# An mLSTM cell with a SwiGLU block behind it: the steps of the beginning in another order, and the last group's results stored in token order

## The chip, the cores and the metric

One core of one Trainium2 chip. Times are device microseconds. The kernel before took 580.2 us (median of three runs, 579.98 to 581.21). A profile of one execution has a span of 577.6 us from the first to the last instruction; all positions below are microseconds from the start of that span. The profile's names: PE is TensorE (matmul), PEld its weight loads, DVE VectorE, ACT ScalarE, POOL GpSimd, SP the engine that issues most DMAs.

## The reference

The attention part is a recurrence over 768 tokens for 4 x 8 heads of 40 elements; the second part is a SwiGLU block on 3072 tokens of 320 features, with 1536 hidden units.

```python
for t in range(S):                                   # B=4, H=8, S=768, D=40
    m_new  = maximum(f_gate[t] + m, i_gate[t])
    f_stab = exp(f_gate[t] + m - m_new); i_stab = exp(i_gate[t] - m_new); m = m_new
    C = f_stab * C + i_stab * outer(v[t], k[t])      # D x D per head
    n = f_stab * n + i_stab * k[t]
    y[t] = sigmoid(o_gate[t]) * (C @ q[t]) / maximum(abs(n @ q[t]), 1.0)
x = y.transpose(0, 2, 1, 3).reshape(B * S, H * D)    # 3072 x 320
g = x @ w_gate                                       # 320 x 1536
out = (g * sigmoid(g) * (x @ w_val)) @ w_out         # 3072 x 320, float32
```

The three weight matrices come as 64-bit floats, and the kernel turns them into 32-bit ones itself.

## The kernel before

The recurrence is done in chunks of 128 tokens. A *unit* is one chunk of one batch (24 units, 6 per batch), a *group* is three units, 384 tokens; there are eight groups. Every group goes through the SwiGLU block in twelve hidden blocks of 128 columns (`H`), then three output tiles of 128 tokens (`J`).

Every step is a Python generator that records a few instructions each time it is advanced, and a string says in which order the generators are advanced. The instructions then stand in that order on every engine, and each engine works in order. `START` is the string of the beginning: the gates, the attention of the first six units, the loads and conversion of all weights, and the whole SwiGLU block of group 0. Later groups have their own strings, which the change leaves alone.

```python
START = """
bar0 pad2 pad3 R1 R0*4 kq0 kq2 pad4 pad2 pad1 pad0 bar0 C1 kq0 runA decA*2 pad1 runB tgA tgB tgA R1*3 kq0 mp which kq0 M0 T0 kq1 M0 ...
"""                                                  # (cut)

def play(names, streams):
    for name in names.split():
        name, _, n = name.partition("*")
        for _ in range(int(n or 1)):
            next(streams.get(name, iter(())), None)
    for s in streams.values():
        do(s)
```

The steps by name (a number is a unit, or a piece of the weights):

- `runA`, `runB`: the two scans over the gates for the first and the second three chunks (`A` on 128 rows, `B` on 32). `mp`, `ep`: split of the running maxima and of the decays into three bf16 parts. `tgA`, `tgB`: transpose of the gates on TensorE and copy to `g_T`. `decA`, `decB`: the decays between chunks. `which`: small constants. `pad`: memsets of the rings. `store`: maxima and decays to DRAM (`M_dram`, `e_dram`).
- `kq`, `v`, `o`: loads. `bar`, `M`: the maxima of a unit spread over TensorE's accumulators (tile `mb`); `W`: exponentials of them (tile `w_sb`). `w`: the same maxima read from DRAM instead, one broadcast of 512 KB. `T`: transpose of k and q. `E`/`e`: the decays, on TensorE or from DRAM (`e_bc`). `S`: scores (`sp`), times `w_sb`, and q times the decay.
- `P`, `I`: the two parts of y (`yT`). `N`: the new state C (`add`). `F`: division, output gate, and the transpose into `xT`.
- `R`: loads of a piece of the weights into one of five raw buffers; `B`: loads of the "behind" slice, the weight rows of features 32 to 39 of every head, into the end of `h_ring`. `C`: conversion of a piece (two ACT, two DVE, one POOL instruction).

The parts that the change touches, or that the working below needs:

```python
def convert(n):                                       # C
    ...
    nc.scalar.activation(bits, hi.bitcast(F32), AF.Abs, scale=2.0 ** -112)
    nc.scalar.activation(low, lo, AF.Identity, scale=2.0 ** -29, bias=step_c)
    yield
    nc.vector.tensor_scalar(bits, bits, scalar1=3, scalar2=None, op0=ALU.logical_shift_left)
    nc.vector.scalar_tensor_tensor(size, in0=hi, scalar=0x80000000, in1=bits, op0=ALU.bitwise_and, op1=ALU.bitwise_xor)
    yield
    nc.gpsimd.tensor_tensor(place(*key).bitcast(U32), low, size, op=ALU.add)
    yield

def hidden(g, m, i0=0, i1=GC):                        # H
    cols = slice(i0 * L, i1 * L)
    ps = [psum.tile([128, TW], F32, name="gv_ps", tag="gen") for _ in range(2)]
    for kc in range(NKC):                             # 5 slices, the fifth is the "behind" slice
        for i in range(2):
            r = slice(i * HP, (i + 1) * HP)
            nc.tensor.matmul(ps[i][:, cols], lhsT=wgv_sb[r, kc, ts(m, 128)], rhs=xts[g][r, kc, cols], ...)
    yield
    sg = gsp.tile([128, TW], F32, name="sg")
    nc.scalar.activation(sg[:, cols], ps[0][:, cols], AF.Sigmoid if g else AF.Silu)
    yield
    if g:
        nc.vector.tensor_tensor(sg[:, cols], sg[:, cols], ps[0][:, cols], op=ALU.mult)
    nc.vector.tensor_tensor(h_ring[:, (g * NFC + m) % NH, cols], sg[:, cols], ps[1][:, cols], op=ALU.mult)
    yield

def project_last(g, i):                               # last output tile of the last group
    n = DM // 2
    for c, mul in enumerate((nc.scalar.mul, nc.vector.tensor_scalar_mul)):
        p = psum.tile([128, n], F32, name="o_ps", tag="gen")
        for m in range(NFC):
            nc.tensor.matmul(p, lhsT=h_ring[:, (g * NFC + m) % NH, ts(i, 128)], rhs=wo["sb"][:, m, ts(c, n)], ...)
        yield
        z = gsp.tile([128, n], F32, name="z_sb")
        mul(z, p, 1 / TWICE)
        yield
        dst = out[ds(g * TW + i * 128, 128), ts(c, n)].rearrange("(t four) d -> four t d", four=NSQ)
        for r in range(NSQ):
            (nc.sync if r % 2 else nc.scalar).dma_start(out=dst[r], in_=z[r * 32:(r + 1) * 32])
        yield
```

Within a tile of 128 tokens, `xT`, `h_ring` and the results stand in the order "four t": token 0, 4, 8, ..., then 1, 5, ... A store puts the rows back in their places. For group 0, blocks 0 to 2 are done in two parts, of 128 columns (first unit) and of 256 (the other two), so that there are fifteen `H` steps there.

Of the kernel before, what the change touches and what calls it, by code (L numbers as in the profile page):

```python
# [13 lines left out]
ALU = mybir.AluOpType  # L14
# [18 lines left out]
"""  # L33

START = """
bar0 pad2 pad3 R1 R0*4 kq0 kq2 pad4 pad2 pad1 pad0 bar0 C1 kq0 runA decA*2 pad1 runB tgA tgB tgA R1*3 kq0 mp which kq0 M0 T0 kq1 M0 bar1 decB pad0 M1 W0 ep tgB M1 o0 o2 C2 pad5*2 W0 T0*3 store C1 v0 kq1 bar2 pad3 M2 B M2 kq2 o0 v1 W0 R5*3 decB C2 R5 kq1*2 o2 o1 S0 decA o1 C2 store S0 pad4 T1 kq2 v2 B S0 kq2 W1 B*2 decB C1 W1 T2 w3 R2*2 W1 kq3 I0 W2 T1 R2 T2 kq3 kq4 decA R2 G0 F0 C7 G2 N0 decA kq4 R3 kq5*2 decB G0 N0 R4 T1 kq5*2 kq4 decB T1 N1*2 G1 kq4 F0 N1 S1 kq3*2 R3*3 R4*3 C7 W2 F0 G2 S1*2 W2 T2 B F0 E1 T2 C7 F0 W3 C0 S1 S2 C0 W3 B*3 S2 G1 P1 W3 R7 I1 E2 C0 C3 S2 F1 H0 S2 R7 H0 T4 F1 P2 T3 R7 store v3 R7 F1 I2 T4 T3 T5*2 R10 T5 C3 F2 R10 F2 R10 R6 F1 R6 T4 F2 H0 R6 F1 C3 T5 T4 R6 F2 N2 C4 T3 H1 F2 o5 H4 H1 C4 C6 C4 N2 R10 H4 H1 R11 C6 o3 T3 R8 H4 C6 R11*2 H5*2 R11 H2 N2 H2 H5 C5*2 R8 C8 R8 C5 H2 S3 C8*2 C10*2 H7 R8 R9 C10 C13*2 W3 H7 C13 H8 H7 C9 H8 C9 R9 C14 R9 H8 C9 o3 R9 C14 C15 C14 S3 H6*2 H3 H6 N3 C11 R16 C15 H3*2 C11 N3 R18 w4 G3 C15 H10 N3 R17 C11 e3 C12*2 v4 C12 e3 H14 C20 H10 S3 R12 C22 e4*2 S4 R15 C20 H10 R13 W4 H14 C20 C22 W4 H14 W4 H13 G3 H9 W4 o5 R14 H13 H9 S4 C22 o4 C21 H13 H11 C19 S4*2 C21 H9 H11 C21 C16 R19 H12 C19 C16 H11 w5 S3 C19 C17 P3 C16 C17 N4*3 H12 C18*2 C17 C18 C23 I3 G5 W5 v7 C23 w8 e5 S5 W5 C23 e5 v5 W5 G5 X o4 J0 H12 F3 S5 w6 S5*2 J1 W8 X J2 F3 J2 W8 G4 P5 x0 P4 w7 x0*2 F3 I5 X I4 x0*3 F5 v8 J6 v6 x2 x0 J3 F3 J2 F3 W7 G4 W8 X W7 x2 F4 F5 F4*2 x2 F5 W6 W8 W7 x0 F5 J7 x2 J4 x2 x3 F4 W7 k6*2 x1 x2 x1 F4 J8*3 F5 x3 x1 x2 k7 W6 J5 W6 x3 J5*2 x1*2 k7 W6 x1*2 x3 x1 x3 k8*2 x3*3 x2
"""


# [16 lines left out]
def kernel(  # L56
# [25 lines left out]
    nc = tc.nc  # L82
    B, H, S, D = q.shape
# [7 lines left out]
    NFC = DF // 128  # L91
    GC = NB // 2
    TW = GC * L
    HP = 64
    NKC = DM // HP
    NG = 2 * B
# [20 lines left out]
    for c0, c1, quarters in ((0, GC, (0, 2, 3)), (GC, NB, (0,))):  # L117
        for r in quarters:
            for t, a in ((f_sb, f_gate), (i_sb, i_gate)):
                (nc.scalar if r else nc.sync).dma_start(  # L120
                    out=t[r * BH:(r + 1) * BH, c0:c1], in_=a.rearrange("b h (c t) -> (b h) c t", t=L)[:, c0:c1])
# [3 lines left out]
    NSQ = L // 32  # L125
# [6 lines left out]
    NH = NFC + 1  # L132
    h_ring = const.tile([128, NH, TW], F32)
# [86 lines left out]
    X = 2 * D  # L220
    wgv_sb = wpool.tile([128, NKC, DF], F32)
    wo = {}
    N4 = 4
    P4 = DF // N4
# [441 lines left out]
    def hidden(g, m, i0=0, i1=GC):  # L666

        cols = slice(i0 * L, i1 * L)
        ps = [psum.tile([128, TW], F32, name="gv_ps", tag="gen") for _ in range(2)]
        for kc in range(NKC):  # L670
            for i in range(2):
                r = slice(i * HP, (i + 1) * HP)
                nc.tensor.matmul(ps[i][:, cols], lhsT=wgv_sb[r, kc, ts(m, 128)], rhs=xts[g][r, kc, cols],  # L673
                                 start=(kc == 0), stop=(kc == NKC - 1))
# [3 lines that stand above are left out]
        yield  # L678
        if g:
            nc.vector.tensor_tensor(sg[:, cols], sg[:, cols], ps[0][:, cols], op=ALU.mult)  # L680
        nc.vector.tensor_tensor(h_ring[:, (g * NFC + m) % NH, cols], sg[:, cols], ps[1][:, cols], op=ALU.mult)  # L681
        yield

    def project(g, i, part):

        if part == 0:
            tag = "conv" if g and i < 2 else "gen"
            hs[g, i] = psum.tile([128, DM], F32, name="o_ps", tag=tag, bufs=PB[tag])
        p = hs[g, i]
        n = NFC // 3  # L690
        for m in range(part * n, (part + 1) * n):
            nc.tensor.matmul(p, lhsT=h_ring[:, (g * NFC + m) % NH, ts(i, 128)], rhs=wo["sb"][:, m, :],  # L692
                             start=(m == 0), stop=(m == NFC - 1))
        yield
        if part == 2:
            z = gsp.tile([128, DM], F32, name="z_sb")
            nc.scalar.mul(z, p, 1 / TWICE)  # L697
            yield
            nc.sync.dma_start(out=out[ds(g * TW + i * 128, 128), :].rearrange("(t four) d -> four t d", four=NSQ), in_=z)
            yield  # L700

    def project_last(g, i):
# [5 lines that stand above are left out]
                nc.tensor.matmul(p, lhsT=h_ring[:, (g * NFC + m) % NH, ts(i, 128)], rhs=wo["sb"][:, m, ts(c, n)],  # L708
                                 start=(m == 0), stop=(m == NFC - 1))
            yield  # L710
            z = gsp.tile([128, n], F32, name="z_sb")
            mul(z, p, 1 / TWICE)
            yield
            dst = out[ds(g * TW + i * 128, 128), ts(c, n)].rearrange("(t four) d -> four t d", four=NSQ)
            for r in range(NSQ):
                (nc.sync if r % 2 else nc.scalar).dma_start(out=dst[r], in_=z[r * 32:(r + 1) * 32])
            yield


# [45 lines left out]
    for n, b in enumerate(blocks):  # L765
        stream(f"H{n}", hidden, 0, *b)
    for i in range(GC):
        for part in range(3):
            stream(f"J{3 * i + part}", project, 0, i, part)
# [3 lines left out]
    for g in range(1, NG):  # L773
        streams.clear()
        for m in range(NFC):
            stream(f"H{m}", hidden, g, m)
        for n in range(3 * GC):
            if g == NG - 1 and n >= 3 * (GC - 1):
                stream(f"J{n}", project_last, g, GC - 1)
                break  # L780
            stream(f"J{n}", project, g, *divmod(n, 3))
        for n, u in enumerate(group(g + 1)):
            for name, f in (("o", load_o), ("G", gate_o), ("e", load_e), ("S", scores), ("F", finish)):
                stream(f"{name}{n}", f, u)
            tag = "gen" if n < 2 else "cell"
            stream(f"N{n}", newer, u, "conv")
            stream(f"I{n}", within, u, tag, u % NB == 0)
            stream(f"P{n}", before, u, tag, True)
        for n, u in enumerate(group(g + 2)):
            for name, f in (("k", load_k), ("v", load_v), ("w", load_w), ("T", turn_x), ("W", weigh)):  # L790
                stream(f"{name}{n}", f, u)
        if g + 2 < NG:
            for n in range(4):
                stream(f"x{n}", load_x, g + 2, n)
        if g == 1:
            for n, u in enumerate(third):
                stream(f"t{n}", turn_x, u)
        play(GROUP1 if g == 1 else GROUP, streams)
# [30 lines left out]
```

## Time and profile before

| | busy us | share of the span |
|---|---|---|
| TensorE | 559.4 | 97% |
| VectorE | 304.3 | 53% |
| ScalarE | 214.8 | 37% |
| GpSimd | 175.0 | 30% |

The granted clock of TensorE is 0.991 over the span. The beginning (START) lasts until about 114 us, where the last of group 0's output tiles ends and the next group's hidden blocks begin; after it the groups follow each other every 66 to 67 us. By ten microseconds, TensorE's busy time at the beginning and the share of the DMA engines is:

| us | 0-10 | 10-20 | 20-30 | 30-40 | 40-50 | 50-60 | 60-70 |
|---|---|---|---|---|---|---|---|
| PE busy | 4.84 | 7.25 | 7.19 | 8.41 | 8.87 | 8.80 | 10.00 |
| DVE busy | 8.24 | 8.69 | 8.50 | 9.34 | 7.36 | 5.65 | 7.49 |
| DMA share | 0.82 | 1.07 | 0.97 | 1.14 | 0.83 | 0.97 | 0.95 |

In a timeline, a row has the start, the time from the first to the last of the merged instructions, engine, line, operation, tiles out<-in, shape and number; in brackets the idle time of the engine before it and what ended it. In a list of waits, a row has who waited for whom, the sum, the number and the longest. A matmul of 32-bit floats shows as two.

### The profile page before, as it was taken

To read this page: it belongs to the slowest core of one execution; us is meant where nothing else is said; L and a number is where in the kernel's file an instruction comes from. 1 tells how busy PE (TensorE), PEld (TensorE's weight loads), DVE (VectorE), ACT (ScalarE), POOL (GpSimd) and SP (SyncE) were. 2 spreads that over 40 slices of the span, in tenths; PEclk is the share of its full clock that TensorE was granted. 3 is DMA by queue.
4 is the path that set the end of the run, shared out by engine and by line. 5 is a ranking of instruction groups with operands and counts; after the bars stand their busy time and mean duration, and the time that the engine had idled before them with its cause. 6 is when DMAs were issued, how large, how long until landed. Compare 5 with 4: busy or idle time off the path is not lost.

```text
span 577.6 us, 10981 instructions
## 1 busy us (share of the span) xinstructions
PE 559.4 (97%) x4102; PEld 383.6 (66%) x4102; DVE 304.3 (53%) x712; ACT 214.8 (37%) x469; POOL 175.0 (30%) x258
## 2 busy tenths in 40 slices
PE   4879999999999999999999999999999999999997
PEld 2657877666776667766576666766677665765666
DVE  8895768637456455634664445724664343623320
ACT  2986897732244215242154213341153221111100
POOL 5565578801142211511223211331125120210000
PEclk8899999999999999999999999999999999999999
DMA  9998998555551663046610565026700300010001
GB/s 162 179 169 213 274 241 201 82 100 90 60 134 37 124 101 112 11 85 93 128 39 25 110 95 127 28 50 112 141 38 12 112 1 1 5 32 0 1 2 34
DMA packets 158385, 51.43 MB, mean 89 GB/s; under 512 B 136476, under 2 KB 150524, under 8 KB 158204
## 3 DMA queue, kind: packets, MB, share of 16 engines
q1 hardware_dynamic: 157948, 50.46, 42.7%
q8 instruction: 32, 0.52, 0.4%
q10 hardware_dynamic: 384, 0.28, 0.2%
q14 instruction: 21, 0.17, 0.1%
HBM read 46.60 MB, written 4.11 MB: 88 GB/s over the span
## 4 chain that ended last, share of the span: by engine, by line
PE 88%; DMA 6%; SPq 3%; DVE 1%; POOL 1%; issue 1%; ACT 0%; POOLq 0%; DVEq 0%
PE gv_ps L673 52%; PE o_ps L692 25%; PE yT L578 5%; PE sp L559 3%; PE add L604 2%; DMA k<-in_k_dram 2%; DMA q<-in_q_dram 2%; SPq L288 1%; PE o_ps L708 1%; DMA w_sb<-M_dram 1%; SPq L275 1%; DMA v<-in_v_dram 1%; SPq L157 1%; DMA f_sb<-in_f_gate_dram 0%; POOL qT L567 0%
## 5 line engine op out<-in xcount | busy, mean ns | idle before, releaser
L673 PE MATMUL gv_ps<-xT,wgv_sb 64*128 64x384 f32 (+2 forms) x1980 | 317.9, 474 | 1.2 <-POOL wgv_sb L320 1.2
L673 PEld LDWEIGHTS gv_ps<-xT,wgv_sb 64*128 64x128 f32 x1980 | 194.1, 187 | 113.0 <-issue 3.2
L692 PE MATMUL o_ps<-wo_sb,h_ring 128*128 128x320 f32 x552 | 151.0, 434 | 0.0
L680 DVE TENSOR_TENSOR sg<-sg,gv_ps 128x384 f32<-128x384 f32 x84 | 46.5, 554 | 174.1 <-ACT sg L677 174.1
L692 PEld LDWEIGHTS o_ps<-wo_sb,h_ring 128*128 128x128 f32 x552 | 104.1, 190 | 44.1 <-issue 1.7
L677 ACT ACTIVATE sg<-gv_ps 128x384 f32<-128x384 f32 (+2 forms) x99 | 47.4, 479 | 227.2 <-PE gv_ps L673 227.0
L681 DVE TENSOR_TENSOR h_ring<-sg,gv_ps 128x384 f32<-128x384 f32 (+2 forms) x99 | 53.5, 541 | 12.0 <-ACT sg L677 2.9
L645 POOL TENSOR_TENSOR yb<-yb,o 128x512 f32<-128x512 f32 x24 | 30.8, 1285 | 94.1 <-DVE yl L644 93.9
L530 ACT ACTIVATE w_sb<-w_sb,g_T 128x128 f32<-128x128 f32 x168 | 50.8, 388 | 18.5 <-POOL w_sb L526 18.4
L567 POOL TENSOR_TENSOR qT<-qT,e_bc 128x512 f32<-128x512 f32 x18 | 22.9, 1272 | 109.2 <-PE sp L559 63.2
L526 POOL TENSOR_SCALAR_AFFINE_SELECT w_sb<-w_sb 128x1024 f32<-128x1024 f32 x21 | 23.6, 1125 | 55.5 <-DMA w_sb<-M_dram 54.7
L659 DVE STREAM_TRANSPOSE xT<-yb 128x512 f32<-128x512 f32 x24 | 17.1, 711 | 36.6 <-POOL yb L652 27.4
L652 ACT COPY yb<-yb 32x512 f32<-32x512 f32 x24 | 14.8, 615 | 52.3 <-POOL yb L645 52.0
L563 DVE TENSOR_TENSOR w_sb<-sp,w_sb 128x512 f32<-128x512 f32 x48 | 31.0, 682 | 5.7 <-POOL v_w L535 3.8
L559 PEld LDWEIGHTS sp<-qT,kT 64*128 64x128 f32 x384 | 25.4, 188 | 7.5 <-issue 1.9
L214 POOL COPY lo<-o 32x128 f32<-32x128 f32 x48 | 19.3, 403 | 35.3 <-ACT o L211 32.6
L559 PE MATMUL sp<-qT,kT 64*128 64x128 f32 x384 | 26.5, 274 | 1.7 <-DVE C L614 1.1
L578 PE MATMUL yT<-w_sb,v 128*64 128x128 f32 x384 | 26.1, 276 | 0.0
L320 POOL TENSOR_TENSOR wgv_sb<-low,size 128x512 uint32<-128x512 uint32 (+1 forms) x16 | 19.2, 1203 | 13.6 <-DVE size L316 10.0
L578 PEld LDWEIGHTS yT<-w_sb,v 128*64 128x64 f32 x384 | 22.7, 137 | 0.7 <-issue 0.7
L697 ACT ACTIVATE z_sb<-o_ps 128x320 f32<-128x320 f32 x23 | 9.8, 430 | 35.3 <-issue 20.5
L632 DVE STREAM_TRANSPOSE yb<-yT 128x256 f32<-128x256 f32 x48 | 19.0, 428 | 5.2 <-PE yT L578 5.1
(102 smaller groups left out, 407.9 us busy)
## 6 DMA issues: line engine op xcount, KB each, us to landing
w_sb<-M_dram SPq DMA_DIRECT2D x21, 512.0 KB
e_bc<-e_dram SPq DMA_DIRECT2D x36, 128.0 KB
k<-in_k_dram SPq DMA_DIRECT2D x48, 80.0 KB
o<-in_o_gate_dram SPq DMA_DIRECT2D x48, 80.0 KB
v<-in_v_dram SPq DMA_DIRECT2D x24, 160.0 KB
raw<-in_moe_w_out_dram SPq DMA_DIRECT2D x8, 480.0 KB
out_dram<-z_sb SPq DMA_DIRECT2D x23, 160.0 KB
raw<-in_moe_w_gate_dram SPq DMA_DIRECT2D x24, 128.0 KB
```

Source lines behind the costliest of these rows:

```text
L526: nc.gpsimd.affine_select(w, w, compare_op=ALU.is_ge, fill=-NEG, base=0, pattern=[[0, H], [1, L]], channel_multiplier=-1)
L530: nc.scalar.activation(w[:, h], m[h], AF.Exp, bias=g_T[:, c, b * H + h:b * H + h + 1], scale=-1.0)
L559: nc.tensor.matmul(sps[two][:, j, :], lhsT=un["kT"][r, j, :], rhs=un["qT"][r, j, :], start=True, stop=True)
L563: nc.vector.tensor_tensor(w2, un["sp"][two], w2, op=ALU.mult)
L567: (nc.vector if "mb" in un else nc.gpsimd).tensor_tensor(un["qT"], un["qT"], un["e"], op=ALU.mult)
L578: nc.tensor.matmul(un["ys"][two][col * HP:(col + 1) * HP, (h % PR) // 2, :], lhsT=lhsT, rhs=rhs, start=(two, col) in un["fresh"], stop=las ...
L645: nc.gpsimd.tensor_tensor(yb, yb, un["o"].rearrange("p x (four d) -> p x four d", d=D)[:, :, :, 0:32], op=ALU.mult)
L673: nc.tensor.matmul(ps[i][:, cols], lhsT=wgv_sb[r, kc, ts(m, 128)], rhs=xts[g][r, kc, cols], start=(kc == 0), stop=(kc == NKC - 1))
L677: nc.scalar.activation(sg[:, cols], ps[0][:, cols], AF.Sigmoid if g else AF.Silu)
L680: nc.vector.tensor_tensor(sg[:, cols], sg[:, cols], ps[0][:, cols], op=ALU.mult)
L681: nc.vector.tensor_tensor(h_ring[:, (g * NFC + m) % NH, cols], sg[:, cols], ps[1][:, cols], op=ALU.mult)
L692: nc.tensor.matmul(p, lhsT=h_ring[:, (g * NFC + m) % NH, ts(i, 128)], rhs=wo["sb"][:, m, :], start=(m == 0), stop=(m == NFC - 1))
```

## The change

The string `START` is replaced by another order of the same steps. It was made with other durations of the loads than the ones that the old string was made with. In the last group the values `h` are written in token order, so that the rows of a result are already in their places: the result of an output tile goes out in one plain transfer, and each half of the last output tile, which had four transfers on two queues, takes one. The groups before it are as they were.

```diff
 START = """
-bar0 pad2 pad3 R1 R0*4 kq0 kq2 pad4 pad2 pad1 pad0 bar0 C1 kq0 runA decA*2 pad1 runB tgA tgB tgA R1*3 kq0 mp which kq0 M0 T0 kq1 M0 bar1 decB pad0 M1 W0 ep tgB M1 o0 o2 C2 ... (cut)
+pad0 R2 bar0 kq1 pad3 R2 pad5 bar1 R2 kq0 pad0 kq0*2 R1 pad2 kq0 R2 pad1 bar0 runA o0 pad3 v0 R3 decA B pad4 tgA mp
+pad1 pad2 o2 o0 which kq1 tgA M0 T0 runB M0 T0 kq1*2 T0 decA R5*2 decB R5 R1 o1 W0 R5 W0 kq3 o1 M1 W1 decA W0 R1*2 ... (cut)
 """
@@ hidden
-        nc.vector.tensor_tensor(h_ring[:, (g * NFC + m) % NH, cols], sg[:, cols], ps[1][:, cols], op=ALU.mult)
+        h = h_ring[:, (g * NFC + m) % NH, cols]
+        if g < NG - 1:
+            nc.vector.tensor_tensor(h, sg[:, cols], ps[1][:, cols], op=ALU.mult)
+        else:
+            sq = "p (i four t) -> p i four t"
+            nc.vector.tensor_tensor(h.rearrange("p (i t four) -> p i four t", i=i1 - i0, four=NSQ),
+                                    sg[:, cols].rearrange(sq, i=i1 - i0, four=NSQ),
+                                    ps[1][:, cols].rearrange(sq, i=i1 - i0, four=NSQ), op=ALU.mult)
@@ project
-            nc.sync.dma_start(out=out[ds(g * TW + i * 128, 128), :].rearrange("(t four) d -> four t d", four=NSQ), in_=z)
+            dst = out[ds(g * TW + i * 128, 128), :]
+            nc.sync.dma_start(out=dst.rearrange("(t four) d -> four t d", four=NSQ) if g < NG - 1 else dst, in_=z)
@@ project_last
-            dst = out[ds(g * TW + i * 128, 128), ts(c, n)].rearrange("(t four) d -> four t d", four=NSQ)
-            for r in range(NSQ):
-                (nc.sync if r % 2 else nc.scalar).dma_start(out=dst[r], in_=z[r * 32:(r + 1) * 32])
+            nc.sync.dma_start(out=out[ds(g * TW + i * 128, 128), ts(c, n)], in_=z)
```

What the cut hides, in words. In the new order the three-part split (`mp`) and the spread of the first unit's maxima (`M0`) stand ahead of the second scan (`runB`) in VectorE's and TensorE's lists. The weights of hidden block 0 (`R0`), which were loaded first of all, are loaded after the first `w` broadcast; hidden block 1 comes before block 0. The four transposes of the last two first-half units' q (`T4`, `T5`) and the fourth unit's scores (`S3`) come after the first 384-wide hidden blocks. The decays are stored to DRAM (third step of `store`) after all loads of gate and value weights, where before they were stored in their midst.

## The prediction

> **What bounds the kernel now.** I read the page's busy shares and slices first, then TensorE's waits, then the timelines of the first 60 us, then the end.
>
> ```profile
> PE 559.4 (97%) x4102; PEld 383.6 (66%) x4102; DVE 304.3 (53%) x712; ACT 214.8 (37%) x469; POOL 175.0 (30%) x258
> PE   4879999999999999999999999999999999999997
> DMA  9998998555551663046610565026700300010001
> ```
>
> TensorE sets the time. A slice is 14.44 us: only the first three slices and the last fall short of 9. In the first seven slices the DMA engines are busy 80% of the time or more. The waits of TensorE over the whole run are these:
>
> ```profile
> PE tp_g L430 <- DVE i_sb L384: 3.4, 1, 3.4
> PE mb L501 <- DVE f_sb L424: 2.7, 1, 2.7
> PE mb L483 <- DVE keep L326: 1.9, 1, 1.9
> PE tp_kq L544 <- DVE w_sb L563: 1.6, 2, 0.8
> PE gv_ps L673 <- POOL wgv_sb L320: 1.2, 1, 1.2
> PE sp L559 <- DVE C L614: 1.1, 1, 1.1
> ```
>
> With six smaller ones (2.8 us) they come to 14.7 us, all before 56 us. The last matmul ends at 574.1 of the span of 577.6 us. So 14.7 + 3.5 = 18.2 us is all that a new order can touch (577.6 - 559.4 gives the same), and the first 1.9 us and the gate scan cannot go. 2% is 11.6 us. Two stretches carry the argument. The first is the start of the chain of gates, in TensorE's timeline:
>
> ```profile
> 13.28 0.58 PE L501 MATMUL mb<-f_sb,ones_of 128*128 128x128 bf16 x4 [2.71 <-DVE f_sb L424]
> 19.27 1.16 PE L559 MATMUL sp<-qT,kT 64*128 64x128 f32 x16
> 27.80 1.16 PE L559 MATMUL sp<-qT,kT 64*128 64x128 f32 x16 [1.07 <-DVE C L614]
> 38.67 1.09 PE L578 MATMUL yT<-w_sb,v 128*64 128x128 f32 x16
> ```
>
> The second is the last wait of all, for the "behind" slice of the weights (timelines of ScalarE, GpSimd and TensorE):
>
> ```profile
> 53.05 0.52 ACT L311 ACTIVATE bits<-h_ring 128x384 f32<-128x384 f32 x1 [1.47 <-DMA v<-in_v_dram]
> 54.89 0.99 POOL L320 TENSOR_TENSOR wgv_sb<-low,size 128x384 uint32<-128x384 uint32 x1 [4.72 <-DVE size L316]
> 55.94 9.68 PE L673 MATMUL gv_ps<-xT,wgv_sb 64*128 64x384 f32 x64 [1.20 <-POOL wgv_sb L320]
> ```
>
> After 55.94 TensorE never waits again. Whatever is not done on it by then is paid in full; whatever is done is saved.
>
> **What the Trainium skill says.** "DMA: Bandwidth & Descriptors", section "Why a DMA increments its semaphore by 16 and not by 1": the number of DMA engines of a transfer is the largest number up to 16 that divides the slowest dimension of both sides. A result store of before has 4 x 32 rows on the DRAM side, hence 4 engines. The trace agrees: the 128 packets of the store issued at 561.65 begin at 562.84 and end at 565.09, 2.25 us, with about four under way at once. A plain 128-row store should get 16. "ScalarE: Activation LUTs", section "What ACT_TABLE_LOAD costs", gives 1283 ns for the load; the trace has 1.28 us. "TensorE: Matmul & The Clock Gate", Part 1, says that an idle array is throttled; the trace shows a granted clock of 0.50 from 10 to 18 us, behind the two gate waits. No page tells how an order of steps turns out.
>
> **The change part by part.** The new START holds the same work; I laid its order on the measured durations. VectorE is the engine to follow: it is busy 7.4 to 9.3 of every 10 us up to 50 us.
>
> *Gates.* Before, the three-part split of the gate maxima (1.18 us) stands behind the second scan, run B (3.34 us), and ends at 13.23. Now it follows the first half: 8.47 + 0.21 for a memset + 1.18 = 9.86. The spread on TensorE starts about 3.4 us earlier.
>
> *First unit.* Run B now stands between the split and the first kT copy: 9.86 + 0.62 (which) + 0.2 (g_T) + 3.34 = 14.05, copy done at 14.65. ScalarE no longer waits for weights before its first exponential, so qT comes at about 14.6. The first scores go from 19.27 to about 14.7, 4.6 us earlier.
>
> *Then the lead melts.* VectorE does nearly the same list up to the third unit's qT product in both orders: one 384-wide conversion (1.1 us) leaves, the two products for yb and yl (1.1 us) come in. By my walk it now waits for "add" at 19.6 (0.75 us), and at 28.8 and 30.9 (0.4, 0.75, 0.75), and two conversions (2.7 us) stand ahead of the second unit's score products. Second scores: 27.80 to about 23.8. Second qT: 31.8 to 28.1. Third qT: 36.6 to 36.0. End of the third unit's last yT matmuls: 39.7 to about 39.0. Of 4.6 us, 0.7 is left.
>
> *New waits from 39 to 46 us.* The weights of block 0 came in the first eleven transfers; now they are transfers among which the 512 KB w_sb broadcast lies. Adding the packet times of the transfers ahead of their last (0.61 us for half a k or q, 1.23 a v, 0.60 a weight row piece, 1.87 the broadcast: packets times mean packet time over 16 engines) gives 32.3 us. In before, landings after the broadcast lag this sum by 5.7 us (transfer 55 had 26.2 us up to the one eight before it, and its issue waited until 31.9), so about 38.0. Then 0.6 + 0.7 on ScalarE, 0.7 + 0.6 on VectorE, 1.3 on GpSimd: 41.4. Block 0 waits about 1.2 us. The last half of k of the sixth unit lands at 38.4 + 5.8 = 44.2, and its transposes wait about 1.5 us, in order, with everything behind them.
>
> *The gate at 56 us.* The fourth large load of the "behind" slice has 88 transfers up to it in either order, 44.3 us of packet time in both (four k or q halves are swapped for four weight pieces). Each load's issue waits for the landing of the one eight before it, and nothing lets this one land earlier than in before, about 53. Conversion and GpSimd put the release at about 55.9 again. TensorE gets there at 45.4 + 1.1 + 3 x 2.15 + 2.6 = 55.5, so it waits 0.3 instead of 1.2 us. What it has done by then: one 256-wide block more (2.13 us), one score group (0.9) and two q transposes (1.2) less. Sum: even. That is the centre for START: 0, with a little for the smaller wait.
>
> *Later.* e_dram is stored after the weights instead of before, so the first e_bc lands at about 73 and its product on GpSimd at about 74.4, where TensorE needs it at 74.7. I see no wait, but little slack.
>
> *The end.* The last result's four stores of 32 rows on two queues (second ones issued at 574.89, packets until 576.14) become one, issued at 574.53. At the 0.82 us from issue to first packet seen there, and 8 packets of 37 ns on each of 16 engines, it ends at about 575.7 to 575.9: -0.3 us. The 12 products of the last group that now write h in steps of four elements are VectorE's, which sits idle 2.0 us before each block's pair of products there; the last h is written at 556.2 and first read by TensorE at about 560.4 (554.4 + 11 products of 0.545). Nothing on the path.
>
> Sum: 0 at the start, -0.3 from the shorter wait, -0.3 at the end, -0.2 for a TensorE that is throttled less in 8 to 18 us: 580.2 - 0.8 = 579.4 us.
>
> **The rivals.** (1) The early lead survives: the 4 us at the first and second scores reach the end because VectorE waits less than in my walk and the "behind" slice lands earlier. For it: the order was made for durations of loads. Against it: equal transfers ahead of that slice. It would give 576 to 577. (2) New waits win: block 0, the sixth unit's k, and late e_bc each cost more than I say, as TensorE's order is fixed and one late tile blocks all. For it: before waits directly for landings only twice, 1.3 us together; now three waits hang on them. It would give 581.5 to 583. (3) The end is worse: a store of 128 rows takes the 2.25 us of the 4 x 32 one; +1.4 us. Against it: the engine rule above.
>
> **Range and chances.** The walk is good to about 2 us, its terms pulling both ways, and the rivals lie 3 us to either side: 576.8 to 582.2. For more than 2% faster, 11.6 of the 18.2 idle us would have to go, with at least 6 of them fixed: 0.02. For 2% slower TensorE would have to wait about as long again as now: 0.015. Within: 0.965.
>
> **What would show it.** Right: the gate spread near 9.9 us and first scores near 14.7; third unit's last yT near 39; a wait of a gv_ps on wgv_sb near 40 and of a k transpose on its load near 44; the release of the "behind" slice near 56; the last packets before 576 in a span of the old length. Wrong: the "behind" slice released before 54 or after 58; a sum of TensorE's waits under 12 or over 17 us; any wait after 60 us, above all for qT after e_bc.

## The result and the profile after

The changed kernel takes 582.89 us (median of four, 582.72 to 583.07) beside 580.09 us (579.96 to 581.21) for the kernel before: a ratio of 1.0044 [1.0027, 1.0061], slower by 0.4%. The prediction was 579.4 us with a range to 582.2. The profiled execution has a span of 581.1 us (577.6 before); a time is about 1.8 us more than its span.

The page of the changed kernel, busy times and slices (a slice is now 14.53 us), and below it the one line of clocks from the page of the kernel before:

```profile
PE 566.1 (97%) x4102; PEld 385.1 (66%) x4102; DVE 305.7 (53%) x712; ACT 214.9 (37%) x469; POOL 175.0 (30%) x258
...
PE   6879999999999999999999999999999999999997
...
PEclk8579999999999999999999999999999999999999
```
```profile
PEclk8899999999999999999999999999999999999999
```

TensorE has the same 4102 instructions and is busy 6.7 us longer: the same matmuls ran slower. The second and third digits of the clock say where, 14.5 to 43.6 us. The list of TensorE's waits in the changed kernel is shorter than before, not longer:

```profile
PE sp L572 <- DVE kT L561: 2.2, 1, 2.2
PE mb L514 <- DMA q<-in_q_dram: 2.1, 1, 2.1
PE mb L496 <- DVE keep L339: 1.9, 1, 1.9
PE e_ps L525 <- DVE w_sb L576: 1.7, 2, 0.8
PE dec_ps L422 <- DVE w_sb L576: 1.2, 1, 1.2
...
PE tp_kq L557 <- ACT qT L563: 0.7, 1, 0.7
...
PE gv_ps L686 <- POOL wgv_sb L333: 0.2, 1, 0.2
```

With four more of 0.2 to 0.8 us they come to about 12 us, against 14.7; none falls after 50 us, and the "behind" slice no longer stops TensorE. So 2.7 us of waiting went and 6.7 us of busy time came. Windows of the changed kernel, then of the kernel before (busy time and number by engine, then the granted clock, the DMA share and GB/s):

```profile
12.00:30.00 18.00, 13.46 (x101) 10.80 (x99) 15.02 (x33) 13.98 (x29) 8.18 (x14) 0.50 1.06 182
30.00:36.00 6.00, 5.95 (x64) 4.82 (x64) 2.96 (x7) 3.32 (x10) 4.29 (x8) 0.62 0.99 209
36.00:45.00 9.00, 6.49 (x80) 5.40 (x82) 8.01 (x19) 4.77 (x10) 6.20 (x9) 0.81 1.08 155
```
```profile
12.00:30.00 18.00, 13.91 (x135) 11.16 (x135) 15.32 (x40) 15.26 (x37) 8.89 (x15) 0.80 0.98 178
30.00:36.00 6.00, 5.36 (x88) 4.43 (x86) 5.73 (x14) 4.63 (x13) 5.22 (x7) 1.00 1.20 161
36.00:45.00 9.00, 6.92 (x88) 5.30 (x86) 6.80 (x17) 7.35 (x14) 5.05 (x10) 1.00 0.98 173
```

From 12 to 30 us TensorE is busy about as long in both but gets 101 matmuls done instead of 135, at 0.50 of its clock. From 30 to 36 us it is VectorE that has fallen back: 7 instructions instead of 14; of its three waits there, 0.9 to 1.0 us each, two are for TensorE, which hardly rests (5.95 of 6 us), and one is for GpSimd. TensorE's timeline of the changed kernel gives the steps that the prediction put times on:

```profile
10.12 0.39 PE L514 MATMUL mb<-f_sb,ones_of 128*128 128x128 bf16 x4 [2.12 <-DMA q<-in_q_dram]
...
15.42 2.08 PE L572 MATMUL sp<-qT,kT 64*128 64x128 f32 x16 [2.20 <-DVE kT L561]
...
26.52 2.08 PE L572 MATMUL sp<-qT,kT 64*128 64x128 f32 x16 [0.68 <-ACT qT L563]
...
35.88 1.16 PE L572 MATMUL sp<-qT,kT 64*128 64x128 f32 x16
...
42.94 1.95 PE L591 MATMUL yT<-w_sb,v 128*64 128x128 f32 x14
...
46.43 0.83 PE L686 MATMUL gv_ps<-xT,wgv_sb 64*128 64x128 f32 x10 [0.23 <-POOL wgv_sb L333]
```

VectorE's timeline of the changed kernel has the two qT products, which end at 30.88 and 40.05 us (31.8 and 36.6 before):

```profile
30.19 0.69 DVE L580 TENSOR_TENSOR qT<-qT,e_ps 128x512 f32<-128x512 f32 x1 [0.20 <-PE e_ps L525]
...
39.37 0.68 DVE L580 TENSOR_TENSOR qT<-qT,e_ps 128x512 f32<-128x512 f32 x1
```

The first scores are 3.9 us earlier than before, the second 1.3 us, and the third unit is done at 44.89 instead of 39.76. The same sixteen score matmuls take 2.08 us at half clock and 1.16 at full clock. Of the 5.1 us by which the third unit is late, 1.1 are made up until group 0's last output tile, which ends at 118.5 instead of 114.5 us; what follows takes as long as before. At the end the last matmul is 3.0 us before the end of the span instead of 3.5.

### The profile page after: what moved, and what is told of

Read it like the earlier page. It is cut to its first block, busy times and chain, and to the rows that moved or that the text cites. A ratio compares the mean times of both kernels' runs of the same rounds, so it can differ in the third digit from the quotient of the medians.

```text
span 581.1 us, 10989 instructions
## 1 busy us (share of the span) xinstructions
PE 566.1 (97%) x4102; PEld 385.1 (66%) x4102; DVE 305.7 (53%) x712; ACT 214.9 (37%) x469; POOL 175.0 (30%) x258
## 4 chain that ended last, share of the span: by engine, by line
PE 91%; DVE 1%; POOL 0%; issue 0%; ACT 0%; DVEq 0%; POOLq 0%
PE gv_ps L686 53%; PE o_ps L713 26%; PE yT L591 5%; PE sp L572 3%; PE add L617 2%; PE o_ps L730 1%; POOL yb L658 0%; PE tp_kq L557 0%; DVE den L648 0%; DVE xT L672 0%; DVE yb L655 0%; DVE yb L645 0%; DVE size L329 0%; ACT yb L665 0%; DVE yl L657 0%
## 5 line engine op out<-in xcount | busy, mean ns | idle before, releaser
L686 PEld LDWEIGHTS gv_ps<-xT,wgv_sb 64*128 64x128 f32 x1980 | 190.1, 187 | 114.6 <-issue 3.3
L696 DVE TENSOR_TENSOR h_ring<-sg,gv_ps 128x384 f32<-128x384 f32 (+2 forms) x87 | 46.9, 540 | 13.9 <-ACT sg L690 5.7
L572 PEld LDWEIGHTS sp<-qT,kT 64*128 64x128 f32 x384 | 26.7, 199 | 9.3 <-ACT bits L324 2.4
L227 POOL COPY lo<-o 32x128 f32<-32x128 f32 x48 | 19.3, 403 | 39.2 <-ACT o L224 35.7
L572 PE MATMUL sp<-qT,kT 64*128 64x128 f32 x384 | 27.8, 287 | 2.9 <-DVE kT L561 2.2
L591 PE MATMUL yT<-w_sb,v 128*64 128x128 f32 x384 | 28.4, 288 | 0.0
L591 PEld LDWEIGHTS yT<-w_sb,v 128*64 128x64 f32 x384 | 24.5, 144 | 1.1 <-issue 0.9
```

The lines of the kernel that those rows point to most:

```text
L572: nc.tensor.matmul(sps[two][:, j, :], lhsT=un["kT"][r, j, :], rhs=un["qT"][r, j, :], start=True, stop=True)
L591: nc.tensor.matmul(un["ys"][two][col * HP:(col + 1) * HP, (h % PR) // 2, :], lhsT=lhsT, rhs=rhs, start=(two, col) in un["fresh"], stop=las ...
L696: nc.vector.tensor_tensor(h, sg[:, cols], ps[1][:, cols], op=ALU.mult)
```

## The experiments

There were eighteen kernels. Nearly all edits are places of names in the string of the beginning, shown as diffs of the piece around them. "Filled" means repeats of a mask matmul into an accumulator that the real mask overwrites later: more work, the same results. The runs come from six batches, each with the kernel before beside it (medians of 579.65 to 580.12 us); from batch to batch it is the distance to that kernel that can be compared.

```diff
+    def fill(u, half, n):
+        for _ in range(n):
+            nc.tensor.matmul(units[u]["mb"][half], lhsT=ident_b, rhs=late..., start=True, stop=False, ...)
+        yield
```

Theory A at the outset was the clock: the new order breaks TensorE's work up by waits, the array stays at half clock, and the slower matmuls lengthen the exchange between TensorE and VectorE. Theory B was the order itself: something in it holds the second and third unit whatever the clock.

### Which part, and is it the clock

**e1**: the changed kernel, filled in three pauses.

```diff
-pad4 tgA mp ... M1 W1 decA W0 R1*2 store M1 ... F0 S1 kq5
+pad4 tgA fa mp ... M1 W1 decA W0 R1*2 store fb M1 ... F0 S1 fc kq5      (10, 9 and 6 repeats)
```

> The new kernel with 25 repeated matmuls of 128x512 that only rewrite the mask (start=True, before the real sums): 10 before the first gate spread, 9 before the last of the second unit's, 6 after the second unit's scores. They fill TensorE's idle stretches near 8, 13 and 25 us. Theory A, that the new order is slower because TensorE works through 10.7 to 34.6 us at half the clock (in the profile of the new kernel its matmuls there last about twice as long, and VectorE waits for them): the clock is full from about 7 us on, second scores at about 24 instead of 26.5 us, end of the third unit's yT near 40 instead of 44.9, and the time falls by 2 to 4 us, to 579 to 581. Theory B, that the new order's waits for other engines make it slow whatever the clock: time stays at 582.5 to 583.5 (or rises by what the fillers delay).

Measured: 582.11 us (nine), ratio 1.0040 [1.0027, 1.0053]. The filling did not always hold the clock. Its executions, sorted:

| mean clock | spans, us |
|---|---|
| 0.982, 0.985 | 581.6; 580.4, 580.5, 580.8 |
| 0.988 | 579.6, 579.9, 580.3 |
| 0.993, 0.994 | 579.1, 579.1 |

Within one and the same kernel the span falls by 2.5 us as the clock rises by 0.012. The kernel before beside it shows next to nothing of this: 578.0 us (median of 18) at 0.986 and below, 577.8 (nine) at 0.990 and above. So in this run the span goes with the clock, and the two executions at the highest clock are still 1.3 us above the kernel before. Which of the two makes the other is not shown by that: whatever lengthens TensorE's pauses in an execution can lower its clock too.

**e2**: the old string, the new end. **e3**: the new string, the old end.

```diff
 e2: START of the kernel before, hidden / project / project_last of the changed one
 e3: START of the changed kernel, hidden / project / project_last of the one before
```

> The old order of the beginning with the new end (token order, one transfer per result). From the two profiles the end is 0.55 us shorter (from the last result's product on VectorE to the end of the span 2.9 instead of 3.4 us): 579.5. If the beginning and the end act on each other by anything else, more than 0.3 us away from that.

> The new order of the beginning with the old end. The last output tile of group 0 ends at 118.5 instead of 114.5 us in the new kernel, so: 580.1 + 4.0 - 0 = 583.5 to 584.1, if all of the loss is the beginning's.

Measured: e2 579.64 us (twenty), ratio 0.9997 [0.9990, 1.0004]; e3 582.65 us (four), ratio 1.0060 [1.0042, 1.0077]. The end is worth nothing that can be measured, and the whole loss is the beginning's: e3 is 3.0 us above the kernel before beside it, the changed kernel 2.8 us.

**e4**: the kernel before, filled in its two first pauses (15 and 12 repeats).

```diff
-runA decA*2 pad1 runB tgA tgB tgA R1*3
+runA decA*2 pad1 runB tgA fa tgB fb tgA R1*3
```

> The old kernel with 27 such filling matmuls in its two waits for the gates (15 before the second transpose of the gates, 12 before the first spread), where its clock is halved from 8.9 to 19.1 us. Theory A with the release of the behind slice near 56 us as the bound of the old order: full clock from 5 us on, first scores one to two us earlier, but TensorE then waits longer at the behind slice, and the time stays within 0.5 us of 580.1. If the clock is worth its share everywhere: about 1.5 to 2.5 us less. Theory B: no change at all, neither in the first scores.

Measured: 580.93 us (thirteen), ratio 1.0024 [1.0012, 1.0037]: slower, with a clock of 0.993. Its timeline of TensorE:

```profile
17.89 1.16 PE L566 MATMUL sp<-qT,kT 64*128 64x128 f32 x16
...
38.96 1.09 PE L585 MATMUL yT<-w_sb,v 128*64 128x128 f32 x16
...
56.75 3.50 PE L680 MATMUL gv_ps<-xT,wgv_sb 64*128 64x384 f32 x20 [1.72 <-POOL wgv_sb L320]
```

The first scores are 1.4 us earlier, but the lead does not last: the clock is half from 28.9 to 35.7 us, and the third unit is done at 40.05 instead of 39.76. TensorE comes to the "behind" slice at 55.03 instead of 54.74 and waits 1.72 us instead of 1.20, as the slice comes 0.8 us later than before; why, no run tells. So e4 does not show what an early chain of units would be worth in the old order. What a late one costs there can be read from e2, which has the old string and whose profiled execution got a clock of 0.985:

```profile
40.38 1.09 PE L578 MATMUL yT<-w_sb,v 128*64 128x128 f32 x16
...
53.71 6.62 PE L673 MATMUL gv_ps<-xT,wgv_sb 64*128 64x384 f32 x40
```

The third unit is done at 41.47, 1.7 us later than in the kernel before. The wait at the slice is gone, and group 0's last output tile ends at 115.4, only 0.9 us later. So in that execution about half of the delay was taken up, by the wait that the slice would have caused anyway.

### What in the order

VectorE's list ahead of the second unit's score products has two conversions (25.90 to 28.64 us). That was the first suspect, beside the third unit's mask, which the new order records late, ahead of the second scores.

**e5**: mask and spread of the third unit early. **e6**: conversions behind the second unit's two products. **e7**: both. **e8**: both, filled.

```diff
 e5
-C3 S0*2 kq2 ... bar2 R0 N0 ... tgB M2 F0 ... N1 M2 T2
+C3 S0 bar2 M2*2 S0 kq2 ... R0 N0 ... tgB F0 ... N1 T2
 e6
-kq3 C7 R0*2 kq4 C2 W1 R6 C2 T1 S1 kq3 C7 R6 F0 S1 kq5 S1 kq3
+kq3 R0*2 kq4 C2 W1 R6 T1 S1 kq3 R6 F0 S1 kq5 S1 C7 C2 C7 kq3
 e8: e5 + e6, the second half of M2 left late, fa, fb as in e1, fc ahead of the first S1
```

> The changed kernel, with the third unit's mask (1.03 us at half clock) and its spread (0.6 + 0.6 us) moved from ahead of the second scores to TensorE's pause behind the first scores, where the kernel before has them too. No work is added. Clock theory (the loss is TensorE at half clock between 10 and 34 us): the pause at 17.5 us is filled, the second unit's q transposes come 1.6 us earlier; 581 to 582 us, with a clock above 0.98. Order theory (VectorE has two conversions, 2.7 us, ahead of the second unit's score products, which end at 28.6 whatever TensorE does): the second w_sb products still start at 28.6; no gain, 582.4 us or more.

> The changed kernel, with VectorE's two conversions (25.9 to 28.6 us) moved behind the second unit's two score products. Clock theory: the scores themselves end at 28.6 because their matmuls take 2.08 instead of 1.16 us, so the products can't start earlier; 582.5 to 583.2 us. Order theory: the second unit's products, its qT and all behind it come 1 us or more earlier; 581.0 to 581.8 us.

> Both moves of the two runs before in one kernel: third mask and spread early, conversions behind the second unit's products. Clock theory: no more than the first move alone gives, 581 to 582 us. Order theory: the products follow the scores at about 26.9 us, 1.7 us earlier; 580 to 581 us. If each is right for one part: 579 to 580.5 us.

> Both moves, and TensorE's pauses filled with repeats of mask matmuls whose result is overwritten (10, 9 and 6 of them). Both theories together: the clock above 0.99, second scores before 25 us, and 577.5 to 579.5 us, below the kernel before. If it stays at 580 us or more, then neither the clock nor the two conversions is what keeps the new order behind, and what counts is further on (the third unit from 34 us, or the slice of weights landing at 54 us).

Measured: e5 582.04 us (five), 1.0037 [1.0023, 1.0050]; e6 584.06 (four), 1.0073 [1.0055, 1.0092]; e7 584.91 (four), 1.0074 [1.0053, 1.0095]; e8 585.45 (four), 1.0088 [1.0053, 1.0123]. Only e5 went about as one theory said (clock). e6 to e8 were misses of a kind that neither theory had: slower than the changed kernel. The waits of TensorE in e6 name it:

```profile
PE e_ps L525 <- DVE w_sb L576: 2.1, 2, 1.3
...
PE tp_kq L557 <- DVE qT L580: 1.1, 1, 1.1
```

I had put the conversions behind the products, but ahead of the same unit's qT product (31.87 instead of 30.19 us), whose operand holds one of the only two "cell" accumulators. The next transposes need that accumulator. So these three runs do not test what they were made for, and e8's profiled execution, at a clock of 0.994 with full clock until 31.7 us, still ended the third unit at 44.8.

**e9**: e8 with the conversions where the changed kernel has them.

> The changed kernel with the third mask (and half its spread) early and TensorE's pauses filled, but with VectorE's two conversions where the changed kernel has them. Against the run with both moves and the same filling it tells whether moving the conversions did the harm. Clock theory: full clock to 31 us at least; the second products at 27.5, the third scores at 33 to 34 (35.9 in the changed kernel), the third unit's last yT done at 42 to 43 (44.9): 580 to 581 us. If the order of VectorE is what counts, the clock gives nothing as long as the two conversions stand ahead of the products: 582 us or more.

Measured: 581.10 us (ten), ratio 1.0030 [1.0019, 1.0040]; nine of ten executions at 0.991 to 0.994 with spans of 578.8 to 579.7. That lies between what the two theories gave. e9 is 1.4 us above the kernel before beside it; e5, the same order but for half the spread and without filling, is 2.1 us above. e8 differs from e9 in the conversions alone. Its median is 4.4 us higher, but two of its four executions ran at 0.982 and 0.985; the two at 0.994 have spans of 581.0 and 582.3, 2 to 3 us above those of e9.

**e10**: the chain of the second unit first: third mask early, second unit's q transposes ahead of the turned gates, one conversion behind qT and one behind the third kT copy. **e11**: that, filled.

```diff
 e10, on top of e5
-R0 N0 tgB decA F0 B decA B R3 tgB F0 R0 w3 T1 kq3 C7 R0*2 kq4 C2 W1 R6 C2 T1 S1 kq3 C7 R6 F0 S1 kq5 S1 kq3
+R0 T1 N0 tgB decA F0 T1 B decA B R3 tgB F0 R0 w3 kq3 R0*2 kq4 C2 W1 R6 S1 kq3 R6 F0 S1 kq5 S1 kq3
-S1 N1 G2 N1 T2 P1 F0 T2 W2
+S1 C7 N1 G2 N1 T2 P1 F0 T2 C2 C7 W2
```

> The changed kernel, without filling, in an order that puts the chain of the second unit first: third mask early, second unit's q transposes ahead of the turned gates (they then don't wait for the dec copy), and each of the two conversions not ahead of the second unit's products nor of its qT but behind them (one behind qT, one behind the third kT copy). Order theory: second scores at 23.5 (26.5), their products at 25.5 (28.7), the third scores 2.5 us or more earlier than 35.9: 579.5 to 580.5 us. Clock theory: the same matmuls at half clock still; 581.5 us or more.

> The order of the run before with TensorE's pauses filled. Both theories: second scores at 23.5, third scores at 31 to 32.5, last yT of the third unit done before 41 us: 577.5 to 579.5 us, at or below the kernel before. If it isn't under the run without filling by 1 us or more, the clock isn't worth what the runs of the first filled kernel suggested.

Measured: e10 581.56 us (five), 1.0029 [1.0006, 1.0053]; e11 582.27 (four), 1.0048 [1.0033, 1.0063]. The filled one is not under the unfilled one by 1 us but 0.7 us above it: by the measure set ahead, the clock isn't worth what e1 suggested. The second scores came at 24.3 and 24.5, but their products did not follow. VectorE's timeline of e10:

```profile
25.39 0.37 DVE L657 TENSOR_TENSOR yl<-yb,lo 128x128 f32<-128x128 f32 x1
27.91 1.29 DVE L576 TENSOR_TENSOR w_sb<-sp,w_sb 128x512 f32<-128x512 f32 x2 [2.15 <-POOL v_w L548]
```

With the conversions gone VectorE stands idle for 2.15 us, until GpSimd's `v_w`. The reason is in two lines of the kernel: the product overwrites in place what `v_w` of the same unit reads.

```python
nc.gpsimd.tensor_tensor(un["v_w"], un["v"][:, :, 0:D1], w[:, :, L - 1:L].to_broadcast(...), op=ALU.mult)   # W, third step
nc.vector.tensor_tensor(w2, un["sp"][two], w2, op=ALU.mult)                                               # S, products, in place
```

GpSimd in the kernel before, and then in the changed kernel:

```profile
21.91 0.75 POOL L535 TENSOR_TENSOR v_w<-v,w_sb 128x328 f32<-128x328 f32 x1
```
```profile
26.13 1.27 POOL L658 TENSOR_TENSOR yb<-yb,o 128x512 f32<-128x512 f32 x1 [1.28 <-DVE yl L657]
27.36 0.75 POOL L548 TENSOR_TENSOR v_w<-v,w_sb 128x328 f32<-128x328 f32 x1
```

VectorE in the changed kernel, the end of the two conversions and the products:

```profile
27.95 0.69 DVE L329 SCALAR_TENSOR_TENSOR size<-raw,bits 128x512 uint32<-128x512 uint32 x1
28.70 1.29 DVE L576 TENSOR_TENSOR w_sb<-sp,w_sb 128x512 f32<-128x512 f32 x2
```

So in the changed kernel three things that the second unit's products need end side by side: `v_w` at 28.11, the scores at half clock at 28.60, the two conversions at 28.64. Lifting one alone shows the next.

**e12**: the changed kernel once more, for the spread of its executions.

> The changed kernel as it is, for more executions of it: 582.9 us. Clock theory: among its executions the span falls as the mean clock rises, by 1 us or more from 0.976 to 0.985. Order theory: no such slope.

Measured: 582.98 us (four), ratio 1.0061 [1.0046, 1.0076]. All eight executions of the changed kernel: 581.1, 581.4 at 0.976, 582.4 at 0.977, 580.9 to 581.3 at 0.982, 580.4 and 581.1 at 0.985. The direction is the clock's, but eight executions don't settle a slope; and no execution of it reached 0.988. In its profiled one (0.985) the second scores ran at full clock, 25.67 to 26.83, and the products, at 28.43, still stood behind the conversions. Its third unit is done at 44.00, 0.9 us earlier than in the first profile of the same kernel: it has five windows of half clock (3.41 us each) in the beginning where the first has eight.

### GpSimd's product and the load of v

**e13**: e10 with the second unit's `v_w` ahead on GpSimd. **e14**: e11 with the same. **e15**: that alone in the changed kernel.

```diff
-R0 T1 N0 tgB ... kq4 C2 W1 R6
+R0 T1 N0 W1 tgB ... kq4 C2 R6
```

> The chain-first order (581.6 us), with the second unit's v_w product moved on GpSimd from behind the yb product to ahead of the reciprocals' copies, where GpSimd is idle from 20.3 to 24.2 us. GpSimd theory: the second products at 25.8 instead of 27.9, third scores 2 us earlier at 33.3, the third unit's last yT done at 42: 579.3 to 580.2 us. Clock theory alone: no change, 581.2 us or more.

> The same move in the chain-first order with TensorE's pauses filled (582.3 us). All theories together: second products at 25.2 (27.1), third scores at 32 to 33 (35.3), last yT before 41.5 (44.8): 578 to 579.5 us, at or below the kernel before. If still 581 us or more, something else behind 30 us holds the order.

> The changed kernel with that one move on GpSimd. If three limits lie side by side there (scores at half clock done at 28.6, the conversions on VectorE done at 28.6, v_w done at 28.1), taking one away gives nothing: 582.5 to 583.2 us. If GpSimd alone were the cause: 581 us or less.

Measured: e13 581.02 us (twenty), 1.0019 [1.0011, 1.0027]; e14 581.56 (seventeen), 1.0038 [1.0026, 1.0050]; e15 583.72 (five), 1.0062 [1.0042, 1.0081]. e15 had no gain, as three limits side by side would have it (its interval overlaps the changed kernel's). e13 and e14 are 1.3 and 1.8 us above the kernel before, e10 and e11 were 1.9 and 2.6. That is less than expected and, by itself, within the intervals; in the profiles the second products come at 26.31 (e13) instead of 27.91 (e10), and the third unit is done at 42.86 instead of 43.97. GpSimd in e14 says what stood behind:

```profile
24.25 0.75 POOL L555 TENSOR_TENSOR v_w<-v,w_sb 128x328 f32<-128x328 f32 x1 [3.94 <-DMA v<-in_v_dram]
25.06 0.42 POOL L660 COPY den<-den 32x16 f32<-32x16 f32 x2
```

`v_w` cannot start before 24.25: its v has not landed. The new order issues that load as transfer 39 (stores counted), at 19.05 us; the kernel before as transfer 31, at 15.23.

**e16**: e13 with the second unit's v loaded eleven transfers earlier (issued at 13.2 us). **e17**: e14 with the same.

```diff
-kq1*2 T0 decA R5*2 decB ... M1 v1 T0 B
+kq1*2 T0 decA v1 R5*2 decB ... M1 T0 B
```

> The kernel with v_w ahead (581.0 us, not filled), with the second unit's v loaded eleven transfers earlier. If the late v is what still held it: v_w done by 23 us (25.0), second products at 25.0 to 25.5 (26.5), the third unit 1 us earlier: 579.5 to 580.3 us. If the chain behind 30 us (third unit's v_w at 34.1 us, its products, C and the last yT) sets the end: no change, 580.7 us or more.

> The same with TensorE's pauses filled (581.6 us without the earlier v). If v held it: 580 us or less. If the chain behind 30 us sets the end: 581 us or more.

Measured: e16 580.43 us (twenty), ratio 1.0016 [1.0006, 1.0026]; e17 580.96 (eighteen), 1.0032 [1.0020, 1.0045]. e16 is 0.7 us above the kernel before beside it, where the changed kernel is 2.8 and 3.3 us above, without any filling. The earlier load by itself is not clear of noise: e13 was 1.3 us above, with an overlapping interval. VectorE's and TensorE's timelines of e16 show the second products at 25.42 instead of 28.70, and the third unit's end at 42.95 instead of 44.89 (e13 had 42.86 already):

```profile
25.42 1.29 DVE L576 TENSOR_TENSOR w_sb<-sp,w_sb 128x512 f32<-128x512 f32 x2
```
```profile
33.34 1.18 PE L572 MATMUL sp<-qT,kT 64*128 64x128 f32 x16
...
41.00 1.95 PE L591 MATMUL yT<-w_sb,v 128*64 128x128 f32 x14
```

The clock still parts its spans: 579.5 us (median of nine, 0.979 to 0.985) against 578.1 (median of eleven, 0.988 to 0.991). The kernel before beside it has 578.1 (fifteen, at 0.985 and below) and 577.9 us (twenty-one, at 0.988 and above). At the same cut e13 has 579.45 and 579.1, e18 (below) 580.5 and 580.6; the kernel before is 0.1 to 1.0 us apart in the six batches. So how much a span goes with the clock differs from run to run, and the new order doesn't stand out in all of them.

e17, at 0.994 for most executions, is not faster than e16: its filling takes TensorE's time too, and the next tie shows, a wait of 2.20 us for the third unit's products.

```profile
34.77 0.42 PE L532 MATMUL e_ps<-e_sb,ones_of 128*64 128x128 bf16 x8 [2.20 <-DVE w_sb L583]
```

**e18**: on top of e16, `v_w` of the third unit ahead of two conversions on GpSimd, its products ahead of the second unit's division on VectorE.

```diff
-T2 C2 C7 W2 B T2 F0 W2 C2 T2 I1 S2 W2 F1 S2 F1 E2 S2
+T2 C2 W2 B T2 F0 W2*2 C7 C2 T2 I1 S2*2 E2 S2 F1*2
```

> The unfilled kernel with v loaded earlier (580.4 us; spans of 577.6 to 580.1), with the third unit's v_w product ahead of two conversions on GpSimd and its two score products ahead of the second unit's transposes and division on VectorE. If that chain sets the end: third qT at 36 instead of 37, the last yT 0.7 to 1.2 us earlier, 579.2 to 579.8 us, level with the kernel before or just under it. If the clock or later work of VectorE decides: 580.2 us or more.

Measured: 582.40 us (eleven), ratio 1.0042 [1.0028, 1.0055]: a miss. The products came at 32.9, but I had left the third qT product behind the division:

```profile
37.92 1.13 PE L591 MATMUL yT<-qT,C 64*64 64x128 f32 x16 [3.26 <-DVE qT L580]
```

So it doesn't tell what the third unit's chain would give with both moved. No version with the new string beats the kernel before.

Filled against unfilled, by the distance to the kernel before: e1 against the changed kernel 0.4 us less, e9 against e5 0.7 less, e11 against e10 0.7 more, e14 against e13 and e17 against e16 0.5 more. As filling costs time too, this neither shows nor excludes a gain by the clock.

## Why the prediction was wrong

| step, us | predicted | before | after |
|---|---|---|---|
| first gate spread | 9.9 | 13.28 | 10.12 |
| first scores | 14.7 | 19.27 | 15.42 |
| second scores | 23.8 | 27.80 | 26.52 |
| second qT done | 28.1 | 31.8 | 30.88 |
| third qT done | 36.0 | 36.6 | 40.05 |
| third unit's last yT done | 39.0 | 39.76 | 44.89 |
| wait of block 0 on its weights | 1.2 | none | 0.23 |
| wait at the sixth unit's k transposes | 1.5 | none | 0.67, for a copy of ScalarE |
| group 0's last output tile done | as before | 114.5 | 118.5 |
| from the last matmul to the end | 3.2 | 3.5 | 3.0 |

**Gates and first unit: right**, to 0.2 and 0.7 us.

**"Then the lead melts": this is the step that failed.** It said "of 4.6 us, 0.7 is left" at the third unit's end; it is 5.1 us late instead. The error against the walk grows from 2.7 us at the second scores to 2.8 at the second qT, 4.0 at the third qT and 5.9 at the end of yT. The waits that I had added behind it came out 1.8 us smaller (0.9 instead of 2.7), and 5.9 - 1.8 = 4.1 is about the 4.0 us by which group 0's last output tile is late. Two things were missing in the walk:

- *GpSimd's list.* I called VectorE "the engine to follow" and counted its two conversions ahead of the second products. That `v_w` has to be done before the in-place product, that the new order puts it behind the yb product, and that v itself is loaded eight transfers later, is not in the walk.
- *The durations of TensorE's steps.* I took them from rows of the kernel before that stand, from 19 us on, at full clock. In the profile of the changed kernel the clock is half from 10.7 to 34.6 and again from 41.4 to 44.8 us. The second scores start at 26.52 there, and at 25.67 in e12's profile, the same kernel.

What each is worth, as far as the runs tell:

| kernel | third unit done, us (clock of that execution) | median above the kernel before beside it, us |
|---|---|---|
| changed; e12, the same; e3, same string | 44.89 (0.976); 44.00 (0.985); 43.53 (0.985) | 2.8; 3.3; 3.0 |
| e5, third mask early | 43.71 (0.982) | 2.1 |
| e10, second unit's chain first | 43.97 (0.982) | 1.9 |
| e13, `v_w` ahead too | 42.86 (0.985) | 1.3 |
| e16, v loaded earlier too | 42.95 (0.982) | 0.7 |
| e17, e16 filled | 42.48 (0.994) | 1.3 |

**The -0.2 for "a TensorE that is throttled less in 8 to 18 us": wrong in sign** in the profiled execution. I counted the half clock of the first pauses and did not ask what happens behind them. The old order goes on at 13.3 us with six microseconds of unbroken, dense work and is back at full clock at 19.1. The new one goes on earlier, but with pauses of 2.2, 0.8, 0.7 and 0.8 us, and gets the clock back at 34.6 (in e12's profile for 3.4 us at 13.0 and for 6.8 us at 23.2). The -0.3 "from the shorter wait" has no ground in the walk itself, which had the slice released at the same time and the work done by then even.

**New waits from 39 to 46 us: right in place, too large.** (The conversion steps after 38.0 add up to 41.9, not 41.4, which makes the forecast wait larger still.) With the units ahead of them later, TensorE met these loads later; rival 2, that new waits win, fell by its mechanism although the time lies in its range. Rival 1, that the lead survives, fell too. e_bc did not stop TensorE: no wait after 50 us.

**The gate at 56 us: wrong.** I expected TensorE at 55.5, a wait of 0.3 us and even work. It came to that matmul at 60.7, 5.2 us later, and did not wait; GpSimd converted the slice at 58.4 to 60.5. ScalarE took the slice up at 56.45 without a wait for its load, in the course of its list, and in e16 the conversion came 1.9 us earlier along with the units. So nothing fixed stands there any more that takes up part of what the chain of units loses, as the wait in the old order does (e2): in e16 the third unit is 1.9 us earlier than in the changed kernel, and group 0's last output tile 2.0 us.

**The end: right in the span**, 3.5 to 3.0 us; in time no gain is shown, between -0.6 and +0.2 us (e2's interval). The rival of a slower store fell: the 128 packets of the first such store take 0.59 us (566.56 to 567.15) where they took 2.25, with about twelve under way at once instead of four.

Shown are: the beginning alone makes the loss (e3), and the moves of e16 (second unit's chain, third mask, two conversions, `v_w`, one load) leave 0.7 us of it, clear of the changed kernel's 2.8 and 3.3, without filling. Five moves stand in e16, and the steps between them lie within each other's intervals. What stays open: how the loss divides between clock and order, as the moves also raise the clock, the three limits of the second products lie within 0.6 us of each other, and filling costs time of its own. Nor is the whole error of the walk explained: of the 5.1 us by which the third unit is late, 0.9 to 1.4 go with the clock between executions of the same string, e16 takes off 1.9 in all, and 3.2 remain there. The third unit's own ties were not told apart (e18).

## What to carry to other kernels

When an order of steps is walked by hand, walk all engines: an in-place product waits for every reader of what it overwrites, on whatever engine and behind whatever load. Ask at which clock a step will run in the new order: here the same sixteen score matmuls took 1.16 or 2.08 us. And ask which wait closes a stage: in front of it a loss costs less (1.7 us became 0.9 in the old order), and once the wait is gone it counts in full (1.9 and 2.0 us in the new one).

## What the runs showed of the hardware

The clock turned over in steps of 3.41 us in every trace. The Trainium skill, "TensorE: Matmul & The Clock Gate", Part 1, gives a free-running window of 3413 ns, and full clock after one busy window. The traces agree with the length: the first stretches of half clock, 10.24 (before) and 23.89 us (after), are three and seven of them. With the second they do not agree, if busy is what the profile counts as TensorE's busy time:

- Two windows of half clock in the changed kernel are busy to the last, 20.93 to 24.34 and 31.17 to 34.58 us (3.41 of 3.41 us each). After the first the clock stayed at half, after the second it was full. The second has no matmul of more than 128 columns, so wide matmuls are not what it takes. What makes the difference was not tested.
- Windows of nearly the same busy time went both ways: 25.93 to 29.34 us in the kernel before (1.96 of 3.41 us) kept the full clock, 37.99 to 41.40 us in the changed kernel (1.99 of 3.41 us) was followed by half clock.
- The same kernel got different clocks from execution to execution, 0.979 to 0.991 for e16, so that one profile is not enough to read a beginning by.
- VectorE's product of 128 x 384 32-bit floats took 848 instead of 554 ns where it is written in steps of four elements, as twelve runs of 32; the step and the short runs were not told apart (VectorE's groups by shape in the changed kernel; the last group's twelve products are L700):

```profile
L696 DVE TENSOR_TENSOR h_ring<-sg,gv_ps 128x384 f32<-128x384 f32 x81 | 44.9, 554 | 12.6 <-ACT sg L690 4.7 <-DVE sg L693 0.5
...
L700 DVE TENSOR_TENSOR h_ring<-sg,gv_ps 128x384 f32<-128x384 f32 x12 | 10.2, 848 | 1.2
```

VectorE has room there, and e2 shows no cost of it.
